# Moving the low halves of the exponentials and of the gated product from GpSimd to VectorE

## The chip, the cores and the metric

The kernel runs on one core of one Trainium2 chip. The time is the device time of one execution in microseconds (us); lower is better. Beside it the profile gives the span, from the first to the last instruction of the program. In the views, PE is TensorE's matmuls, PEld its weight loads, DVE is VectorE, ACT is ScalarE, POOL is GpSimd and SP is SyncE, from whose queue most transfers are issued. L561 is line 561 of the kernel.

## The reference

Three layers follow each other. All inputs and outputs are float32.

```
def phi(x):                                   # x: q or k, 8 batches, 8 heads, 576 rows, 64 wide
    proj = einsum('bhsd,df->bhsf', x, w_phi)  # 128 features
    proj = proj - max(abs(proj), axis=-1)
    return concatenate([exp(proj), exp(-proj)])
q_p, k_p = phi(q), phi(k)
kv, z = einsum('bhsf,bhsd->bhfd', k_p, v), sum(k_p, axis=2)
attn = einsum('bhsf,bhfd->bhsd', q_p, kv) / (einsum('bhsf,bhf->bhs', q_p, z)[..., None] + 1e-6)

x = attn as (4608 tokens, 512)
x = ((x @ w1) * (x @ w2)) @ w3 @ w_out        # d_ff = 1024

e = argmax(x @ w_gate)                        # one of 8 experts for each token
out = softmax(x @ w_gate)[e] * (relu(x @ e_w1[e]) @ e_w2[e])
```

## The kernel before

Every matmul operand is kept as two float16 halves. The high half is the rounded value and the low half is what rounding left, so that three float16 matmuls (high by high, high by low, low by high) stand for one precise product.

**Stages.** Up to about 1225 us the kernel does attention, the gated layer and the preparation of all weights side by side; after that come the experts, where PE has nearly all the work. In the first part four units (pairs of batches) are taken in turn. For each unit there are four calls of `group` (two heads each, attention) and, behind them in due time and beside the next unit's attention, three of `x_prep` and `moe1` (the gated layer, 384 tokens each). The integer arithmetic that turns the raw 64-bit weights into float32 (`conv64`, L214 to L218) runs up to about 190 us.

**The order.** Each step is filed with a due time from the table `O` (`k_lo=0.75`, `q_lo=8.3`, `g_lo=1.2` and so on) and the steps are issued in that order. A scheduler under the kernel then arranges the queue of each engine, by its own estimate of how long each instruction takes and of when its operands are ready. Each engine works through its own queue strictly in order, and semaphores hold an instruction until its operands are there.

**The steps that matter here.** `exp16` (L554, L556) writes an exponential twice on ACT: as float16 into `hl[:, 0]` (tiles `k1`, `q1`, `q2`) and as float32 into `e1`, of which there are three buffers. `exp_lo` (L561) subtracts the one from the other and writes the low half `hl[:, 1]`. It is called 18 times in a group, 6 for the keys and 12 for the queries. In `moe1`, `g_mul` (L817, DVE) multiplies the two projections into `gf`, `g_hi` (L821, ACT) rounds it into `gt`, and `g_lo` (L824) writes the low half; there are 8 of each in a call of `moe1`.

Around them on DVE stand `k_max` (L566), `k_sub` (L572) and `q_max` (L644), which read matmul results from PSUM; `split` (L491, L493), which makes the halves of the queries and keys; `k_c2` (L609), `v_lo` (L540), and the low half of the experts' weights (L325). In `q_add`, L711 and L712 take the numerators `nm` out of PSUM into `nx`; in `q_x`, L719, L720, L721 and L723 divide by the denominators. The PSUM tiles `nm`, `pv` (L521), `pk`, `pq`, `pe` and others share one buffer (tag `ts`, one slot), so that PE can begin on the next only when DVE has read the one before.

```
V.tensor_tensor(nx[:, h], nm[:, :, 0, :], w[:, h].unsqueeze(2).to_broadcast([P, 3, D + 1]), op=ALU.mult)
V.tensor_tensor(nx[:, h], nx[:, h], nm[:, :, 1, :], op=ALU.add)
V.tensor_tensor(rec, nx[:, :, :, D:D + 1], st["ep"][:, :, 3 * c:3 * c + 3].unsqueeze(3), op=ALU.add)
```

Of the kernel before, what the change touches and what calls it, by code (L numbers as in the profile page):

```python
# [14 lines left out]
ALU = mybir.AluOpType  # L15
# [49 lines left out]
def kernel(  # L65
# [16 lines left out]
    V, A, G, T = nc.vector, nc.scalar, nc.gpsimd, nc.tensor  # L82
# [386 lines left out]
    def group(ui, g, T0):  # L469
# [4 lines left out]
        st = {}  # L474
# [83 lines left out]

        def exp_lo(key):
            hl, e1 = st[key]  # L560
            G.tensor_tensor(hl[:, 1], e1, hl[:, 0], op=ALU.subtract)  # L561

        def k_max(h, c):
            if c == 0:
# [162 lines left out]
        for h in range(2):  # L727
            tv = T0 + 3 * h
            for fn in (v_load, v_norm, v_sum, v_scale, v_hi, v_lo, k_s1, k_s2, k_s3, kv_hi, kv_lo):
                at(tv + O[fn.__name__], fn, h)  # L730
            for c in range(3):
                tk = T0 + 3 * h + c
                at(tk + O["k_proj"], proj, "kf", h, c)
                for fn in (k_max, k_sub, k_exp, k_c1, k_c2, k_b):
                    at(tk + O[fn.__name__], fn, h, c)
                at(tk + O["k_lo"], exp_lo, ("k1", h, c))
        for c in range(3):
            tq = T0 + c
            at(tq + O["k_split"], split, "kf", c)
            at(tq + O["k_trans"], trans, "kf", c)  # L740
            at(T0 + O["q_sc"] * c + O["q_split"], split, "qf", c)
            at(T0 + O["q_sc"] * c + O["q_trans"], trans, "qf", c)
            for h in range(2):
                at(T0 + O["q_proj"] + O["q_pc"] * c + O["q_proj_h"] * h, proj, "qf", h, c)
                at(T0 + O["q_max"] + O["q_pc"] * c + O["q_proj_h"] * h, q_max, c, h)
                th = tq + O["q_h"] * h
                for z in range(2):
                    at(th + O["q_lo"] + O["q_lo_z"] * z, exp_lo, ("q", c, h, z))
                for fn in (q_pj, q_exp, q_nm, q_add):
                    at(th + O[fn.__name__], fn, c, h)  # L750
            at(tq + O["q_x"], q_x, c)
# [41 lines left out]
    def moe1(p, c, tk, s):  # L793
# [3 lines left out]
        st = {}  # L797
        gT = []
# [22 lines left out]
            A.copy(gT[m][:, 0, :], st["gf", m])  # L821

        def g_lo(m):
            G.tensor_tensor(gT[m][:, 1, :], st["gf", m], gT[m][:, 0, :], op=ALU.subtract)  # L824

        cw = 256 if last else 260

# [118 lines left out]
        for m in range(8):  # L946
            t = tk + m * s
            at(t, ab, m, 0)
            at(t + 0.5 * s, ab, m, 1)
            for fn in (a_out, g_mul, g_hi, g_lo):  # L950
                at(t + O[fn.__name__], fn, m)
# [278 lines left out]
```

## Time and profile before

| | before |
|---|---|
| median of 3 runs | 1670.81 us (1669.16 to 1676.45) |
| the profiled execution | 1671.89 us |
| its span | 1670.1 us |
| mean granted TensorE clock | 0.943 of full speed |
| PE busy | 1429.4 us, 86% of the span |
| DVE busy | 971.0 us, 58% |
| ACT busy | 885.9 us, 53% |
| POOL busy | 587.5 us, 35% |

The shares are means over two unlike parts. Before 1225 us DVE and PE are both busy for most of the time and POOL for some 40%; behind it only PE is.

### The profile page before, as it was taken

How to read it: one execution, taken by the hardware profiler on the slowest of the kernel's cores; microseconds unless marked ns; L12 is line 12 of the kernel's file. 1: busy time of each engine (PE TensorE's matmuls, PEld its weight loads, DVE VectorE, ACT ScalarE, POOL GpSimd, SP SyncE). 2: the span in 40 equal slices, each digit the busy share in tenths (PEclk: the TensorE clock that was granted, in tenths of full speed). 3: DMA queues.
4: the chain of work that ended last, by engine and by line, in shares of the span. 5: the costliest groups of instructions: out<-in, count | busy, mean ns of one | idle time of the engine just before them, and what ended most of it. 6: DMA issues, size and time to landing. Idle time of an engine off the chain costs nothing. (4 is left out here: it accounts for less than half of the span.)

```text
span 1670.1 us, 38442 instructions
## 1 busy us (share of the span) xinstructions
PE 1429.4 (86%) x14854; PEld 1029.5 (62%) x14854; DVE 971.0 (58%) x2647; ACT 885.9 (53%) x1979; POOL 587.5 (35%) x875
## 2 busy tenths in 40 slices
PE   5888868889897688977787989978949999999998
PEld 4655545656565465756465757646647777777776
DVE  6999989968878687777786886532421111111111
ACT  4787798766776567767576777433311111111111
POOL 3546553444543425434344354211312111121110
PEclk9998978989999799989988999979979999999999
DMA  6756255554257653493955464974347345646361
GB/s 198 217 143 170 64 142 124 144 150 146 71 152 124 127 157 92 119 157 89 161 157 89 139 121 112 140 248 102 70 145 188 83 77 174 221 130 173 76 172 31
DMA packets 273044, 225.17 MB, mean 135 GB/s; under 512 B 187221, under 2 KB 244825, under 8 KB 271706
## 3 DMA queue, kind: packets, MB, share of 16 engines
q1 hardware_dynamic: 265306, 202.71, 50.8%
q0 software_dynamic: 7552, 19.97, 4.1%
q8 instruction: 118, 1.93, 0.5%
q14 instruction: 68, 0.56, 0.1%
HBM read 261.22 MB, written 53.67 MB: 189 GB/s over the span
## 5 line engine op out<-in xcount | busy, mean ns | idle before, releaser
L806 PE MATMUL pab<-xT,w 128*128 128x384 f16 x768 | 263.5, 343 | 8.7 <-DVE gf L817 5.6
L1132 DVE SCALAR_TENSOR_TENSOR hT<-ph,hT 128x512 f16<-128x512 f32 x80 | 55.3, 691 | 362.0 <-ACT hT L1131 362.0
L807 PE MATMUL pab<-xT,w 128*128 128x384 f16 x768 | 262.8, 342 | 0.0
L808 PE MATMUL pab<-xT,w 128*128 128x384 f16 x768 | 262.6, 342 | 0.0
L1127 PE MATMUL ph<-xTb,wb 128*128 128x128 f16 x1280 | 218.1, 220 | 22.5 <-DMA xTb<-rw 22.5
L1128 PE MATMUL ph<-xTb,wb 128*128 128x128 f16 x1280 | 218.1, 220 | 0.0
L1129 PE MATMUL ph<-xTb,wb 128*128 128x128 f16 x1280 | 218.1, 220 | 0.0
L843 PE MATMUL py<-w,gt 128*128 128x260 f16 (+1 forms) x1728 | 205.5, 275 | 12.4 <-ACT yb L850 9.2
L561 POOL TENSOR_TENSOR q<-e,q 128x384 f16<-128x384 f32 x192 | 188.7, 992 | 65.1 <-ACT e L556 60.8
L843 PEld LDWEIGHTS <-gt 128*128 128x128 f16 x1728 | 166.3, 99 | 36.4 <-issue 9.3
L824 POOL TENSOR_TENSOR gt<-gf,gt 128x384 f16<-128x384 f32 x96 | 96.2, 1003 | 182.0 <-ACT gt L821 176.6
L561 POOL TENSOR_TENSOR k<-e,k 128x384 f16<-128x384 f32 x96 | 96.4, 1004 | 159.3 <-ACT k L554 89.3
L702 PE MATMUL nm<-kvs,q 128*128 128x65 f16 (+1 forms) x1920 | 90.1, 204 | 70.2 <-DVE nx L712 35.9
L1131 ACT ACTIVATE hT<-ph 128x512 f16<-128x512 f32 x80 | 47.8, 597 | 187.1 <-PE ph L1129 187.1
L1127 PEld LDWEIGHTS <-wb 128*128 128x128 f16 x1280 | 125.8, 98 | 27.7 <-DMA xTb<-rw 21.2
L702 PEld LDWEIGHTS <-q 128*128 128x128 f16 (+1 forms) x1920 | 79.0, 107 | 100.1 <-issue 47.3
L325 DVE SCALAR_TENSOR_TENSOR pc<-wf,ess,pc 128x512 f16<-128x512 f32 x128 | 104.6, 834 | 47.2 <-ACT pc L321 47.0
L1128 PEld LDWEIGHTS <-wb 128*128 128x128 f16 x1280 | 125.8, 98 | 4.5
L554 ACT ACTIVATE q<-pjT,nM 128x384 f16<-128x384 f32 x192 | 114.4, 596 | 26.0 <-PE nm L702 19.6
L1129 PEld LDWEIGHTS <-wb 128*128 128x128 f16 x1280 | 125.8, 98 | 0.0
L1150 ACT ACTIVATE ob<-pob,scb 128x512 f32<-128x512 f32 x40 | 27.5, 688 | 183.4 <-PE pob L1148 183.4
L626 PE MATMUL kv<-vs,k 128*128 128x65 f16 x1920 | 90.6, 198 | 37.5 <-ACT k L604 23.3
(255 smaller groups left out, 3483.6 us busy)
## 6 DMA issues: line engine op xcount, KB each, us to landing
wb<-wscr SPq DMA_DIRECT2D x40, 4096.0 KB
wf<-in_moe_w_dram SPq DMA_DIRECT2D x16, 2048.0 KB
wscr<-pc SPq DMA_DIRECT2D x128, 256.0 KB
raw<-in_moe_w_dram SPq DMA_DIRECT2D x32, 512.0 KB
rows_d<-row SPq DMA_DIRECT2D x32, 256.5 KB
kf<-in_k_dram SPq DMA_DIRECT2D x64, 128.0 KB
vf<-in_v_dram SPq DMA_DIRECT2D x64, 128.0 KB
qf<-in_q_dram SPq DMA_DIRECT2D x64, 128.0 KB
```

The source lines that it names most:

```text
L325: V.scalar_tensor_tensor(pc[:, 1, :], st["wf"][:, j * 512:(j + 1) * 512], st["s"][:, 0:1], pc[:, 0, :], op0=ALU.mult, op1=ALU.subtract)
L554: A.activation(hl[:, 0], src, AF.Exp, scale=sgn * ES, bias=bias)
L561: G.tensor_tensor(hl[:, 1], e1, hl[:, 0], op=ALU.subtract)
L702: T.matmul(nm[p0:p1, t, z, :], lhsT=hl[:, a, t, p0:p1], rhs=st["kvs"][:, b, h, z, bb, :], start=(a == b), stop=bool(a), skip_group_check=True)
L806: T.matmul(ps, lhsT=wh, rhs=xT[:, 0, kk], start=(kk == 0), stop=False)
L807: T.matmul(ps, lhsT=wh, rhs=xT[:, 1, kk], start=False, stop=False)
L808: T.matmul(ps, lhsT=wl, rhs=xT[:, 0, kk], start=False, stop=(kk == 3))
L824: G.tensor_tensor(gT[m][:, 1, :], st["gf", m], gT[m][:, 0, :], op=ALU.subtract)
L843: T.matmul(py, lhsT=gT[i][:, a, t * P:(t + 1) * P], rhs=w34[:, i, b, hf, 0:cw], start=(i == 0 and a == b), stop=bool(i == 7 and a))
L1127: T.matmul(ph[:, mm, :], lhsT=wh, rhs=xT[:, 0, kk, :], start=(kk == 0), stop=False)
L1128: T.matmul(ph[:, mm, :], lhsT=wh, rhs=xT[:, 1, kk, :], start=False, stop=False)
L1129: T.matmul(ph[:, mm, :], lhsT=wl, rhs=xT[:, 0, kk, :], start=False, stop=(kk == 3))
```

## The change

The two subtractions are issued by VectorE and no longer by GpSimd. Operands, shapes, due times and buffers stay as they are.

```
         def exp_lo(key):
             hl, e1 = st[key]
-            G.tensor_tensor(hl[:, 1], e1, hl[:, 0], op=ALU.subtract)
+            V.tensor_tensor(hl[:, 1], e1, hl[:, 0], op=ALU.subtract)
...
         def g_lo(m):
-            G.tensor_tensor(gT[m][:, 1, :], st["gf", m], gT[m][:, 0, :], op=ALU.subtract)
+            V.tensor_tensor(gT[m][:, 1, :], st["gf", m], gT[m][:, 0, :], op=ALU.subtract)
```

The scheduler arranges the queues of all engines anew. DVE's queue in the first group, where the first numerators `nm_984` and `nm_1041` are taken out of PSUM (the number behind a name is that of the tile, the same in both programs). Before:

```order
L711 TENSOR_TENSOR nx_1018<-nm_984,wq_880 128x195
L638 SCALAR_TENSOR_TENSOR kvs_672<-kv_759,kvs_672 128x130 x2
L712 TENSOR_TENSOR nx_1018<-nx_1018,nm_984 128x195
L566 TENSOR_REDUCE mk_1025<-pj_1003 128x3
L572 TENSOR_TENSOR pm_1036<-pj_1003,mk_1025 128x384
L711 TENSOR_TENSOR nx_1018<-nm_1041,wq_880 128x195
L712 TENSOR_TENSOR nx_1018<-nx_1018,nm_1041 128x195
```

The same place in the changed kernel:

```order
L711 TENSOR_TENSOR nx_1018<-nm_984,wq_880 128x195
L561 TENSOR_TENSOR q1_1010<-e1_1012,q1_1010 128x384
L712 TENSOR_TENSOR nx_1018<-nx_1018,nm_984 128x195
L566 TENSOR_REDUCE mk_1025<-pj_1003 128x3
L217 SCALAR_TENSOR_TENSOR cx_1027<-w12_91,cx_1027 128x512
L572 TENSOR_TENSOR pm_1036<-pj_1003,mk_1025 128x384
L218 SCALAR_TENSOR_TENSOR w12_91<-w12_91,cx_1027 128x512
L561 TENSOR_TENSOR q2_1014<-e1_1016,q2_1014 128x384
L711 TENSOR_TENSOR nx_1018<-nm_1041,wq_880 128x195
L566 TENSOR_REDUCE mk_1025<-pj_1125 128x3
L712 TENSOR_TENSOR nx_1018<-nx_1018,nm_1041 128x195
```

Two of the moved instructions now stand among the six that empty the two `nm` tiles, one of them inside the pair L711 and L712.

POOL's queue at the same exponentials, before:

```order
L561 TENSOR_TENSOR q2_961<-e1_963,q2_961 128x384
L214 TENSOR_SCALAR cx_1180<-raw_909 128x512
L561 TENSOR_TENSOR q1_1010<-e1_1012,q1_1010 128x384
L533 MEMSET vs_1389 128x10
L534 MEMSET vs_1389 128x10
L561 TENSOR_TENSOR q2_1014<-e1_1016,q2_1014 128x384
```

In the changed kernel POOL goes from the conversions straight to the fills of `vs_1389`:

```order
L214 TENSOR_SCALAR cx_1027<-raw_831 128x512
L533 MEMSET vs_1389 128x10
L534 MEMSET vs_1389 128x10
```

DVE's queue in the third unit, where attention and the gated layer run side by side (`gf_10749` is a gated product, `gt_10773` its halves, `pc` are the experts' weights). Before:

```order
L817 TENSOR_TENSOR gf_10749<-pab_10684,asb_10644 128x384
L711 TENSOR_TENSOR nx_10697<-nm_10723,wq_10250 128x195
L325 SCALAR_TENSOR_TENSOR pc_10714<-wf_10071,ess_10650,pc_10714 128x512
L712 TENSOR_TENSOR nx_10697<-nx_10697,nm_10723 128x195
L325 SCALAR_TENSOR_TENSOR pc_10775<-wf_10071,ess_10650,pc_10775 128x512
L719 TENSOR_TENSOR rec_10753<-nx_10697,epq_10251 128x6
```

The same place in the changed kernel:

```order
L817 TENSOR_TENSOR gf_10749<-pab_10684,asb_10644 128x384
L325 SCALAR_TENSOR_TENSOR pc_10714<-wf_10071,ess_10650,pc_10714 128x512
L711 TENSOR_TENSOR nx_10697<-nm_10723,wq_10250 128x195
L561 TENSOR_TENSOR k1_10744<-e1_10746,k1_10744 128x384
L712 TENSOR_TENSOR nx_10697<-nx_10697,nm_10723 128x195
L824 TENSOR_TENSOR gt_10773<-gf_10749,gt_10773 128x384
L719 TENSOR_TENSOR rec_10753<-nx_10697,epq_10251 128x6
```

The low half of the product stands five rows behind the product itself, and a key's low half stands between L711 and L712.

## Rows read from the trace of the kernel before

**Rows 1.** The page's busy time, share of the span, and instructions.

```profile
PE 1429.4 (86%) x14854; PEld 1029.5 (62%) x14854; DVE 971.0 (58%) x2647; ACT 885.9 (53%) x1979; POOL 587.5 (35%) x875
```

**Rows 2.** Busy time of each engine by stretches of the span (columns named).

```profile
core 0: us, PE busy (x) PEld busy (x) DVE busy (x) ACT busy (x) POOL busy (x), PEclk, DMA share, GB/s
50.00:350.00 300.00, 247.77 (x2482) 168.94 (x2483) 275.11 (x699) 235.97 (x544) 144.92 (x224) 0.90 0.56 147
350.00:1050.00 700.00, 578.48 (x6304) 421.37 (x6302) 534.81 (x1517) 484.96 (x1127) 305.18 (x468) 0.94 0.57 124
```

**Rows 3.** Groups of POOL's instructions: count, busy us, mean ns, idle before.

```profile
L561 POOL TENSOR_TENSOR q<-e,q 128x384 f16<-128x384 f32 x192 | 188.7, 992 | 65.1 <-ACT e L556 60.8 <-issue 1.8
L561 POOL TENSOR_TENSOR k<-e,k 128x384 f16<-128x384 f32 x96 | 96.4, 1004 | 159.3 <-ACT k L554 89.3 <-ACT e L556 69.3
L824 POOL TENSOR_TENSOR gt<-gf,gt 128x384 f16<-128x384 f32 x96 | 96.2, 1003 | 182.0 <-ACT gt L821 176.6 <-issue 5.1
```

**Rows 4.** POOL's busy time (and count) by stretches: twice line 561, then line 824.

```profile
50.00:350.00 300.00, 95.19 (x92) 0.90 0.56 147
350.00:1050.00 700.00, 185.19 (x192) 0.94 0.57 124
350.00:1050.00 700.00, 64.12 (x64) 0.94 0.57 124
```

**Rows 5.** Who waited for whom: us in total, times, longest.

```profile
PE nm L702 <- DVE nx L712: 35.9, 14, 7.5
PE pv L521 <- DVE nx L712: 22.3, 12, 4.1
PE nm L702 <- POOL q L561: 7.0, 12, 1.2
```

**Rows 6.** One tile's instructions: duration ns minimum, median, maximum.

```profile
L572 DVE TENSOR_TENSOR pm<-pj,mk x96: 508/546/558, 27.5 to 1004.4; 128x384 f32<-128x384 f32 x96
L712 DVE TENSOR_TENSOR nx<-nx,nm x96: 339/347/359, 82.0 to 1047.5; 128x195 f32<-128x195 f32 x96
L719 DVE TENSOR_TENSOR rec<-nx,epq x48: 148/167/4601, 86.0 to 1048.2; 128x6 f32<-128x6 f32 x48
L540 DVE SCALAR_TENSOR_TENSOR vs<-vf,vss,vs x32: 870/880/3096, 36.8 to 1003.6; 128x640 f16<-128x640 f32 x32
```

**Rows 7.** Groups of DVE's instructions: count, busy us, mean ns, idle before.

```profile
L719 DVE TENSOR_TENSOR rec<-nx,epq 128x6 f32<-128x6 f32 x48 | 28.9, 601 | 0.8
L540 DVE SCALAR_TENSOR_TENSOR vs<-vf,vss,vs 128x640 f16<-128x640 f32 x32 | 32.8, 1024 | 1.5 <-ACT vs L532 1.4 <-DMA vf<-in_v_dram 0.2
```

**Rows 8.** Timeline at 438 us, DVE and POOL: start, us, instruction.

```profile
438.80 4.60 DVE L719 TENSOR_TENSOR rec<-nx,epq 128x6 f32<-128x6 f32 x1
438.98 1.79 POOL L561 TENSOR_TENSOR q<-e,q 128x384 f16<-128x384 f32 x2
...
441.59 1.78 POOL L561 TENSOR_TENSOR q<-e,q 128x384 f16<-128x384 f32 x2
```

**Rows 9.** Timeline from 575 to 582 us, DVE, POOL and PE.

```profile
575.12 1.34 DVE L493 SCALAR_TENSOR_TENSOR sp<-qf,sp 128x192 f16<-128x192 f32 x2
575.18 2.05 POOL L561 TENSOR_TENSOR q<-e,q 128x384 f16<-128x384 f32 x2 [0.31 <-ACT e L556]
576.66 0.54 DVE L566 TENSOR_REDUCE mk<-pj 128x3 f32<-128x384 f32 x1
577.12 0.34 DVE L712 TENSOR_TENSOR nx<-nx,nm 128x195 f32<-128x195 f32 x1
577.61 0.46 PE L521 MATMUL pv<-ssv,ones 128*128 128x1 f32 x2 [4.12 <-DVE nx L712]
579.16 0.53 PE L808 MATMUL pab<-xT,w 128*128 128x384 f16 x1
580.68 0.62 DVE L493 SCALAR_TENSOR_TENSOR sp<-kf,sp 128x192 f16<-128x192 f32 x2
581.72 0.33 PE L808 MATMUL pab<-xT,w 128*128 128x384 f16 x1
```

## The prediction

> **What bounds the kernel now.** I read the totals first. PE is busy for 86% of the span, DVE for 58%, POOL for 35% [rows 1]; over the whole span no engine but PE seems short of time. The table by stretches corrects that [rows 2]. Between 50 and 350 us DVE is busy for 275.1 of 300 us (92%) and PE for 247.8 (83%), at a granted clock of 0.90. Between 350 and 1050 us DVE is busy for 534.8 of 700 us (76%) and PE for 578.5 (83%) at 0.94. So while attention runs DVE is the fullest engine first and the second fullest later, and the moved work lands on it.
>
> Then I read whom PE waits for. The two longest waits that concern this change are for L712, the instruction that empties the shared PSUM slot: 35.9 us in 14 waits before `nm` and 22.3 us in 12 before `pv`, together 58.2 us [rows 5]. For the instructions to be moved PE waits little: 7.0 us in 12 waits for L561 [rows 5]. GpSimd's own lateness is therefore not what holds the kernel. What it does to DVE may be.
>
> That shows in the durations. L719 handles 6 numbers in a row of a tile; its shortest takes 148 ns, its median 167, its longest 4601 [rows 6]. At the longest, DVE starts L719 at 438.80 us, GpSimd runs five L561 from 438.98 to 443.37, and L719 ends at 443.40 [rows 8]: it stood until the last of them was done. L712 and L572, which take one operand from PSUM, never take more than 359 and 558 ns [rows 6]. So an instruction of DVE with its operands in SBUF can be held by GpSimd, one that reads PSUM is not. The Trainium skill (SBUF — State Buffer, "Who interferes with whom") says that a VectorE instruction with two SBUF inputs and a GpSimd instruction that reads SBUF exclude each other; this trace agrees, with 4601 against 167 ns.
>
> **What the change does, part by part.** *Removed from GpSimd*: 192 + 96 + 96 = 384 instructions, 188.7 + 96.4 + 96.2 = 381.3 us [rows 3]. GpSimd is no bound, so that by itself is worth only part of the 7.0 us above.
>
> *Added to DVE*: the same 384. The trace has no such instruction on DVE. The nearest is L572, also a subtraction of two operands over 128x384: 546 ns from start to end, 508 at least [rows 6]. When something is ready behind an instruction of this length the next starts sooner: L566 (as long) starts at 576.66 and L712 at 577.12, 0.46 us later, though L566 lasts 0.54 [rows 9]. Bounds: 384 x 0.46 = 177 us and 384 x 0.55 = 211 us. DVE mostly has work queued, so I take 0.48 us, which is 184 us. The Trainium skill (VectorE: DVE Perf Modes, "The DRAIN you can't avoid") has the next instruction wait until the pipeline is empty; by that the upper bound would be the price, 211 us, against my 184. The two rows above, which overlap by 0.08 us, speak for the lower.
>
> *Given back to DVE*: the holding ends. I take for each group the mean less the median, times the count. L719: (601 - 167) x 48 = 20.8 us; L540, the smallest of ten groups that I counted: (1024 - 880) x 32 = 4.6 us [rows 6, 7]. The eight between (L493 for queries and for keys, L325, L721, L723, L609, L491 twice) come by the same working to 79 us, together 104 us, or 0.27 us for each instruction moved. The bounds are 0 (if what stays on GpSimd, such as the conversions and the indirect transfers, did the holding) and some 130 us (with the small groups). I take 104, since in the two stretches of timeline that I show it is L561 that holds.
>
> *Sum for DVE*: 184 - 104 = +80 us of work, between 177 - 130 = +47 and +211. It falls mostly into two stretches. From 50 to 350 us stand 92 L561 and some 8 L824, from 350 to 1050 us 192 and 64 [rows 4]. At +0.21 us each (0.48 - 0.27) that is +21 us on 275.1, which makes 296 of 300, and +54 us on 534.8, which makes 589 of 700.
>
> *What of it reaches the end.* Before 350 us DVE would have nearly no gap left. If its gaps could close, nothing would be lost; if its share stayed at 92% (275.1 of 300), the stretch would take 296 / 0.917 = 323 us, 23 longer. I take about half, +10 us. Behind 350 us DVE has gaps, and the question is what happens where PE waits. The timeline at 575 to 582 us shows such a place [rows 9]. Two L493 take 1.34 us at 575.12 while GpSimd runs two L561; L712, which nothing holds, comes late behind them, and PE stands for 4.12 us. At 580.68 two L493 take 0.62 us, so GpSimd costs DVE 0.7 us here; on DVE the two subtractions cost 2 x 0.48 = 1.0 us. Nothing is won. At 438 us five of them hold DVE for 4.4 us and would cost 2.4 [rows 8]; there something is won. Where GpSimd's instructions meet PSUM readers, 0.48 us is simply added. Of PE's 58.2 us of waits for L712 [rows 5] I let a tenth go, -6 us, and of its 7.0 us for L561 one half, since the subtraction takes 0.55 us in place of 0.99: -4 us.
>
> A long stand costs PE more than itself. After the 4.12 us the same matmul takes 0.53 us at 579.16 and 0.33 at 581.72 [rows 9]: PE ran at its lower level (1.2 of 2.4 GHz) in between. I count nothing for it, since nearly as many long stands should stay.
>
> The in-order queue is the last part. GpSimd could wait for ACT without harm; 60.8, 89.3 + 69.3 and 176.6 us of its idle time end with ACT [rows 3]. The same wait on DVE holds what stands behind: in the changed queue L712 stands behind a subtraction that needs ACT, and PE waits for L712. I cost it at nothing, because ACT's exponential is filed well ahead and DVE runs late rather than early; if that cover is gone each wait is paid in full by PE's next use of the PSUM slot.
>
> Sum: +10 - 6 - 4 = 0. The profiled execution took 1671.9 us, 1.1 above the median of the runs (1670.8). I predict **1672 us**.
>
> **The rivals.** *Forecast: it cancels*, 1660 to 1684 us, chance 0.40. For it: the sum above, and the place at 575 us.
>
> *Rival 1, slower: DVE becomes the bound.* Place: 50 to 350 us, and every `nm` behind it. Price: +23 us in the first stretch when DVE's share stays at 92%; behind it, if a quarter of the +54 us lengthens the waits for L712, +13 us, less 10 us won: 1672 + 26 = about 1698; with the lower end of the added work (+47 in place of +80) about 1687. I put it at 1692. It decides as soon as DVE cannot close its gaps between 50 and 350 us. For it: 92% is much, and the price 0.55 would add 27 us. Against it: a held DVE is late by microseconds at a time, a busy one by half of one. Chance 0.33. The skill's drain rule is a case of this rival (DVE's work grows by 107 in place of 80 us; the first stretch by 7 more, some 1679), within its chance and, by the overlapping rows, not likelier than 0.05.
>
> *Rival 2, faster: the long holdings were the cause.* If half of the 58.2 us goes (29 us) and the half-speed stretches behind them shrink (a 4 us stand is followed by some 3.4 us at half speed, 1.7 us lost; ten fewer, 17 us, of which I take a third), with 4 us from L561 and +10 us lost early: 1672 - 29 - 6 + 6 = about 1645. For it: one L719 of 4.60 us. Against it: the place at 575 us. Chance 0.27.
>
> That the change does not do what it says is no rival: the queues show the subtractions on DVE and gone from GpSimd.
>
> **How the numbers follow.** A measurement of this kernel can tell about 0.5%, 8 us: below 1662 faster, above 1679 slower. The forecast's 0.40 I split 0.10 below, 0.22 within, 0.08 above. Faster 0.27 + 0.10 = 0.37; same 0.22; slower 0.33 + 0.08 = 0.41. The range reaches into both rivals until 2 in 10 are left out: 1642 to 1702. The ends of the unknown costs lie outside it (+211 us if nothing is given back, all of it at the end: 1883), because PE, not DVE, is the fuller engine behind 350 us.
>
> **What would show it.** Right: 384 subtractions on DVE at 0.5 to 0.56 us; L719's mean near its median; DVE about 80 us busier in all; PE's waits for L712 between 45 and 65 us. Rival 1: DVE above 96% between 50 and 350 us, ACT waiting for L561 to free `e1` buffers, longer waits for L712. Rival 2: waits for L712 below 35 us and a clock above 0.95 in both stretches. Wrong altogether: if the newly arranged queues of PE or SP, which I did not cost, move a step of the gated layer or a transfer by more than all this.

## The result and the profile after

The change made the kernel faster: 1648.6 us (median of 4 runs, 1648.2 to 1653.9) against 1673.6 us for the kernel before on the same chip (4 runs, 1669.2 to 1677.6). The ratio is 0.9862, 95% interval 0.9843 to 0.9882. I had forecast 1672 us, no change to speak of.

The later runs were on chips on which the kernel before takes 1651 to 1654 us, so each run there is compared by its ratio to the kernel before on the same chip, and traces only with traces of equal footing.

The page of the changed kernel, busy time, share of the span and instructions:

```profile
PE 1428.4 (86%) x14850; PEld 1032.2 (62%) x14854; DVE 1001.4 (61%) x3031; ACT 881.7 (53%) x1979; POOL 226.9 (14%) x491
```

Beside [rows 1], POOL lost 360.6 us and DVE gained only 30.4, where I had summed +80. PE's busy time is the same; the profiled execution (1653.9 us, span 1652.2) is shorter because PE idles less.

The stretches (columns as in [rows 2]):

```profile
50.00:350.00 300.00, 253.65 (x2494) 176.65 (x2496) 275.30 (x786) 235.34 (x543) 45.26 (x121) 0.86 0.51 134
350.00:1050.00 700.00, 593.54 (x6424) 429.19 (x6422) 573.88 (x1852) 496.67 (x1161) 74.78 (x220) 0.94 0.66 132
```

Between 50 and 350 us DVE's share stayed where it was, 275.3 of 300 us; between 350 and 1050 us it rose from 534.8 to 573.9. PE's clock did not rise: 0.86 and 0.94, after 0.90 and 0.94.

The moved instructions, and L719 and L723 that stand beside them (groups of DVE's instructions, then one tile's durations in ns):

```profile
L561 DVE TENSOR_TENSOR q<-e,q 128x384 f16<-128x384 f32 x192 | 106.1, 556 | 18.4 <-ACT e L556 17.9
L561 DVE TENSOR_TENSOR k<-e,k 128x384 f16<-128x384 f32 x96 | 54.0, 562 | 22.9 <-ACT e L556 20.6 <-ACT k L554 2.0
L824 DVE TENSOR_TENSOR gt<-gf,gt 128x384 f16<-128x384 f32 x96 | 52.9, 551 | 20.8 <-ACT gt L821 19.9 <-issue 0.6
```

```profile
L719 DVE TENSOR_TENSOR rec<-nx,epq x48: 152/159/166, 87.5 to 1023.9; 128x6 f32<-128x6 f32 x48
L723 DVE TENSOR_TENSOR xn<-nx,rec x48: 544/552/1012, 89.2 to 1025.8; 128x384 f32<-128x384 f32 x48
```

A subtraction takes 551 to 562 ns on DVE, as the 546 ns of L572 had suggested. L719 never takes more than 166 ns now; before it took up to 4601 [rows 6]. The new waits for ACT that I had costed at nothing are there (17.9 + 20.6 + 19.9 us of DVE's idle time), and they did not decide. PE's waits for L712 (us in total, times, longest):

```profile
PE nm L702 <- DVE nx L712: 37.4, 18, 15.8
PE pv L521 <- DVE nx L712: 2.0, 2, 1.8
```

Together 39.4 us, after 58.2 [rows 5]: nearly all of the waits before `pv` went. PE's waits for the moved instructions on POOL, 7.0 us for L561 [rows 5], are gone.

Other waits moved as well, and by as much. Before, PE waited at `kv`, the product of keys and values, for the halves of the keys' second exponential (L604 on ACT, L609 on DVE):

```profile
PE kv L626 <- ACT k L604: 23.3, 7, 14.4
PE kv L626 <- DVE k L609: 9.4, 10, 1.7
```

In the changed kernel these fell from 32.7 to 6.1 us, and three waits that were nearly absent before came up:

```profile
PE kv L626 <- DVE k L609: 3.2, 6, 1.2
PE kv L626 <- ACT k L604: 2.9, 5, 1.6
PE pab L806 <- ACT asb L813: 16.1, 5, 7.1
PE pj L547 <- DMA Tkf<-sp: 10.9, 2, 6.2
PE pj L547 <- ACT e L556: 9.9, 4, 5.4
```

### The profile page after: what moved, and what is told of

It reads as the page before. It is cut to its first block, busy times and chain, and to the rows that moved or that the text cites. A ratio compares the mean times of both kernels' runs of the same rounds, so it can differ in the third digit from the quotient of the medians.

```text
span 1652.2 us, 38216 instructions
## 1 busy us (share of the span) xinstructions
PE 1428.4 (86%) x14850; PEld 1032.2 (62%) x14854; DVE 1001.4 (61%) x3031; ACT 881.7 (53%) x1979; POOL 226.9 (14%) x491
## 5 line engine op out<-in xcount | busy, mean ns | idle before, releaser
L806 PE MATMUL pab<-xT,w 128*128 128x384 f16 x768 | 258.8, 337 | 26.1 <-ACT asb L813 16.1
L807 PE MATMUL pab<-xT,w 128*128 128x384 f16 x768 | 258.8, 337 | 0.0
L808 PE MATMUL pab<-xT,w 128*128 128x384 f16 x768 | 258.3, 336 | 0.0
L843 PE MATMUL py<-w,gt 128*128 128x260 f16 (+1 forms) x1728 | 213.6, 278 | 16.5 <-ACT yb L850 12.1
L843 PEld LDWEIGHTS <-gt 128*128 128x128 f16 x1728 | 166.6, 100 | 43.3 <-issue 13.3
L702 PE MATMUL nm<-kvs,q 128*128 128x65 f16 (+1 forms) x1920 | 86.7, 201 | 41.3 <-DVE nx L712 37.4
L1146 PE MATMUL pob<-wb,hT 128*128 128x512 f16 x320 | 121.3, 379 | 0.0
L1147 PE MATMUL pob<-wb,hT 128*128 128x512 f16 x320 | 121.3, 379 | 0.0
L1148 PE MATMUL pob<-wb,hT 128*128 128x512 f16 x320 | 121.3, 379 | 0.0
L321 ACT ACTIVATE pc<-wf,ess 128x512 f16<-128x512 f32 x128 | 88.8, 726 | 57.2 <-DMA wscr<-pc 50.1
L556 ACT ACTIVATE e<-pjT,nM 128x384 f32<-128x384 f32 x192 | 116.0, 604 | 5.8 <-DVE q L561 5.8
L702 PEld LDWEIGHTS <-q 128*128 128x128 f16 (+1 forms) x1920 | 76.9, 104 | 66.1 <-issue 38.0
```

The lines of the kernel that those rows point to most:

```text
L556: A.activation(e1, src, AF.Exp, scale=sgn * ES, bias=bias)
L702: T.matmul(nm[p0:p1, t, z, :], lhsT=hl[:, a, t, p0:p1], rhs=st["kvs"][:, b, h, z, bb, :], start=(a == b), stop=bool(a), skip_group_check=True)
L806: T.matmul(ps, lhsT=wh, rhs=xT[:, 0, kk], start=(kk == 0), stop=False)
L807: T.matmul(ps, lhsT=wh, rhs=xT[:, 1, kk], start=False, stop=False)
L808: T.matmul(ps, lhsT=wl, rhs=xT[:, 0, kk], start=False, stop=(kk == 3))
L843: T.matmul(py, lhsT=gT[i][:, a, t * P:(t + 1) * P], rhs=w34[:, i, b, hf, 0:cw], start=(i == 0 and a == b), stop=bool(i == 7 and a))
```

## Experiments

Three theories were tried. *Holding*: GpSimd's subtractions held DVE's SBUF instructions, and the release of these is the gain. *Order*: the queues were arranged anew, and the gain is an accident of that. *Latency*: PE gets the low halves themselves sooner. All ratios are to the kernel before on the same chip, with the 95% interval.

**Does arrangement alone move the time?** The kernel before with one due time moved:

```
-    k_lo=0.75
+    k_lo=0.85
```

> The kernel before with one due time moved (k_lo from 0.75 to 0.85), engines as they were: the queues are arranged anew and nothing else. Holding theory: within 0.5% of before. Order theory: arrangement alone moves the time by as much as the change did, 1% or more in either direction.

Measured: 1652.3 us, ratio 1.000 (0.9975 to 1.0024). This run does not try the order theory, because nothing was rearranged. Read from the two traces in order of start, TensorE's 14,854 matmuls and weight loads, DVE's 2647 instructions and those of ACT and POOL stand in the same order as in the kernel before, by operation, tile and shape. What the run gives is a second trace of the kernel before, on the chip of the next three runs. The order theory is tried by the runs below, in which the order was kept and the time moved.

**The release by itself.** The kernel before, with GpSimd writing in place of subtracting:

```
-            G.tensor_tensor(hl[:, 1], e1, hl[:, 0], op=ALU.subtract)
+            G.memset(e1, 0.0); G.memset(hl[:, 1], 0.0)
...
-            G.tensor_tensor(gT[m][:, 1, :], st["gf", m], gT[m][:, 0, :], op=ALU.subtract)
+            G.memset(st["gf", m], 0.0); G.memset(gT[m][:, 1, :], 0.0)
```

> The kernel before, with each of the 384 subtractions on GpSimd replaced by two fills on GpSimd (of e1 or gf, and of the low half): the low halves are zeros, a part of the computation that is left out. GpSimd is about as busy, waits for the same things and VectorE gets no new work, but GpSimd no longer reads SBUF. Holding theory: this is the gain of the release alone, at least that of the change: ratio to before 0.97 to 0.985, L719's mean below 200 ns. Order theory: the queues of the other engines stay nearly those of before, so the ratio is within 0.5% of 1.

Measured: 1587.1 us, ratio 0.9615 (0.9593 to 0.9637), 66 us below before and more than I had expected. (The profiled execution took 1577.0 us, 10 less than the median.) GpSimd is still busy for 512 us. Its page, and L719:

```profile
PE 1406.0 (89%) x14854; PEld 1022.8 (65%) x14854; DVE 857.3 (54%) x2647; ACT 881.3 (56%) x1979; POOL 511.9 (32%) x1259
```

```profile
L719 DVE TENSOR_TENSOR rec<-nx,epq x48: 146/159/252, 82.7 to 961.7; 128x6 f32<-128x6 f32 x48
```

DVE executes the same 2647 instructions as before. To compare on one footing I take the run with the shifted due time, which is the kernel before on this chip:

```profile
PE 1425.7 (86%) x14854; PEld 1027.7 (62%) x14854; DVE 965.4 (58%) x2647; ACT 886.1 (54%) x1979; POOL 587.3 (36%) x875
```

DVE's busy time falls from 965.4 to 857.3 us: 108.1 us were holding. PE's waits for L712 fall from 53.2 us (28.5 and 24.7) to 28.8:

```profile
PE nm L702 <- DVE nx L712: 19.4, 13, 5.4
PE pv L521 <- DVE nx L712: 9.4, 8, 1.9
```

The order of the matmuls is nearly that of the kernel before: 52 of 14,854 stand elsewhere, by tile and shape. The order theory expected a ratio within 0.5% of 1 here, so it is refuted as the account of the release. The zeros don't shorten the matmuls: one of L702 takes 190 ns at least and 194 in the median, with them and without. A fill is not free of holding, though. L491, which reads a single tile in SBUF, still takes up to 1430 ns in this run:

```profile
L491 DVE TENSOR_SCALAR sp<-kf x48: 346/360/1430, 11.5 to 859.2; 128x384 f16<-128x384 f32 x48
```

**The change on the same chip.**

> The changed kernel on the chip of this call, for its ratio beside the others and its trace: 0.984 to 0.988 by the first measurement. The two halves of the change alone came to 0.9888 and 0.9885 on another chip; if that holds here, the halves do not add up.

Measured: 1630.8 us, ratio 0.9886 (0.9857 to 0.9915). Its page:

```profile
PE 1431.5 (88%) x14854; PEld 1033.1 (63%) x14854; DVE 1001.1 (61%) x3031; ACT 882.7 (54%) x1979; POOL 228.4 (14%) x491
```

From the fills (857.3) to the change (1001.1) DVE gained 143.8 us for 384 subtractions, 0.37 us each, and the time rose by 1630.8 - 1587.1 = 44 us. So the change is two large terms: -66 us of release and +44 us of added work. (The low halves' arithmetic is absent in the first, so this split is that of two programs, not of one execution. The +44 also holds what the new order does: about 1,500 of the 14,854 matmuls stand elsewhere, and no run parts the two.)

**More work on DVE.** Each subtraction made twice:

```
             V.tensor_tensor(hl[:, 1], e1, hl[:, 0], op=ALU.subtract)
+            V.tensor_tensor(e1, e1, hl[:, 0], op=ALU.subtract)
...
             V.tensor_tensor(gT[m][:, 1, :], st["gf", m], gT[m][:, 0, :], op=ALU.subtract)
+            V.tensor_tensor(st["gf", m], st["gf", m], gT[m][:, 0, :], op=ALU.subtract)
```

> The changed kernel with each moved subtraction made twice on VectorE (the second into e1 or gf, no longer needed): 384 more instructions on VectorE and nothing on GpSimd. My sum counted 0.48 us for each (184 us) and let +10 us reach the end. If added work on VectorE is cheap, as the holding theory now needs: ratio to before 0.985 to 1.0. If VectorE is the bound once it is this full: 1.02 to 1.06. Order theory: no forecast.

Measured: 1767.4 us, ratio 1.0716 (1.0672 to 1.076). This is above the upper of my two brackets. DVE's busy time:

```profile
PE 1481.3 (84%) x14854; PEld 1054.7 (60%) x14854; DVE 1175.4 (67%) x3415; ACT 889.7 (50%) x1979; POOL 227.5 (13%) x491
```

The second 384 cost 174.3 us of DVE and 137 us of the time, three times what the first 384 cost. Added work was cheap for the first 384 and dear for the next; rival 1 was real, one step further on. That it was cheap because DVE had gaps is my reading. The matmuls' order moved here too, in about 1,500 places against the change.

**Holding put back.** The changed kernel, with GpSimd making each subtraction once more, and the same with two fills in its place:

```
             V.tensor_tensor(hl[:, 1], e1, hl[:, 0], op=ALU.subtract)
+            G.tensor_tensor(e1, e1, hl[:, 0], op=ALU.subtract)       # reading
...
             V.tensor_tensor(hl[:, 1], e1, hl[:, 0], op=ALU.subtract)
+            for _ in range(2):
+                G.memset(e1, 0.0)                                     # writing
```

(`gf` in the same way.)

> The changed kernel, and behind each moved subtraction GpSimd makes the same subtraction once more, into the float32 tile that is no longer needed (e1 or gf): GpSimd's 384 reading instructions are back, VectorE keeps its own. Holding theory: VectorE is held again by some 100 us in all, L719's mean is above 400 ns, and the time goes up by 20 to 45 us, to 1670 to 1695 us. Order theory: VectorE's and TensorE's own instructions are those of the changed kernel, so about 1649 us, within 8. Latency theory: 1649 us.

> The same as the run with GpSimd's repeated subtractions, but GpSimd only writes: two fills of the same float32 tile, together about as long as one subtraction, behind the same waits. Holding theory: instructions that only write do not hold VectorE's two-operand ones, L719's mean stays below 250 ns, 1645 to 1660 us. If it is the mere presence of work on GpSimd (or the later release of e1 and gf) that costs, it comes out like the reading run. Order theory: 1649 us, within 8.

Measured: reading 1741.7 us, ratio 1.0532 (1.0497 to 1.0568); writing 1632.8 us, ratio 0.9867 (0.9818 to 0.9915). The reading run costs far more than the 20 to 45 us that I expected, some 110 us above the writing one, and the writing one costs nothing. GpSimd's main groups in the two (the inserted lines shift the numbers by one and two):

```profile
L562 POOL TENSOR_TENSOR e<-e,q 128x384 f32<-128x384 f32 x192 | 203.0, 1065 | 112.1 <-DVE q L561 86.9 <-DVE rec L722 5.9 <-DVE rec L720 5.7
```

```profile
L563 POOL MEMSET e<- 128x384 f32 x576 | 241.1, 427 | 300.7 <-DVE k L561 132.6 <-DVE q L561 91.1 <-DVE vss L194 12.8
```

Two fills are about as long as a subtraction (2 x 0.43 against 1.07 us). The pages, reading and then writing:

```profile
PE 1463.5 (84%) x14854; PEld 1044.0 (60%) x14854; DVE 1154.9 (66%) x3031; ACT 892.7 (51%) x1979; POOL 636.4 (37%) x875
```

```profile
PE 1425.5 (88%) x14854; PEld 1029.9 (63%) x14854; DVE 1007.3 (62%) x3031; ACT 883.6 (54%) x1979; POOL 538.1 (33%) x1259
```

DVE has the same 3031 instructions in both and is busy for 147.6 us more when GpSimd reads. My sign for it, a mean of L719 above 400 ns, did not come: that mean is 170 ns. It was the new subtractions on DVE that were held, with a mean of 754 ns in place of 556:

```profile
L561 DVE TENSOR_TENSOR q<-e,q 128x384 f16<-128x384 f32 x192 | 143.9, 754 | 9.3 <-ACT e L556 8.6 <-issue 0.4
```

What held DVE is GpSimd reading SBUF, not GpSimd working. The later release of `e1` and `gf` is in both runs; it explains no busy time of DVE, and ACT waits for GpSimd to release `e1` for 23.7 us in the reading run and 13.3 us in the writing one. The matmuls stand in the order of the changed kernel in the reading run and within 7 places of it in the writing one. So the order theory, which expected 1649 us (0.986) of the reading run, is refuted as the cause of the gain, and so is the latency theory.

**Parts of the change.** Exponentials alone, the product alone, and two splits (`key[0]` tells keys from queries):

```
+            V.tensor_tensor(hl[:, 1], e1, hl[:, 0], op=ALU.subtract)       # exponentials alone: g_lo stays on G
...
+            V.tensor_tensor(gT[m][:, 1, :], st["gf", m], gT[m][:, 0, :], op=ALU.subtract)   # product alone: exp_lo stays on G
...
+            (V if key[0] == "k1" else G).tensor_tensor(hl[:, 1], e1, hl[:, 0], op=ALU.subtract)   # keys and product
...
+            (G if key[0] == "k1" else V).tensor_tensor(hl[:, 1], e1, hl[:, 0], op=ALU.subtract)   # queries and product
```

> Only the exponentials' low halves (288 instructions) go to VectorE; the product's (96) stay on GpSimd. Holding theory (the gain is that GpSimd's subtractions no longer hold VectorE's SBUF instructions): the 25 us are shared out roughly by instructions, so about -19 us, some 1655 us, and the mean of L719 falls most of the way from 601 ns to 160 ns. Order theory (the gain is an accident of how the queues were arranged anew): no such sharing; anything between 1640 and 1680 us. Latency theory (the gain is that PE gets the low halves sooner): PE's 7 us of waits for L561 go, 1665 us.

> Only the product's low halves (96 instructions) go to VectorE. Holding theory: about -6 us, some 1667 us, and L719's mean stays above 450 ns. Order theory: anything between 1640 and 1680 us. Latency theory: the short tail behind the last attention group gains 1 to 3 us, 1671 us.

> Keys' and product's low halves (192) on VectorE, the queries' (192) on GpSimd. The product's 96 alone gave 0.9885 and all 384 gave 0.9862 and 0.9886. If release is won first and the price of added work grows with VectorE's load: 0.98 to 0.987, better than either. If the halves simply share one gain: 0.988, the same.

> Queries' and product's low halves (288) on VectorE, the keys' (96) on GpSimd: 0.98 to 0.988, between the run with keys and product and the whole change, if it goes by the number of instructions moved. The queries' stand right at q_add and q_x, where L719 was held for up to 4.6 us; if it is the place that counts, this one is the best of the three.

| on VectorE | instructions moved | ratio to before | interval |
|---|---|---|---|
| exponentials | 288 | 0.9888 | 0.9849 to 0.9927 |
| product | 96 | 0.9885 | 0.9847 to 0.9923 |
| keys and product | 192 | 0.9887 | 0.9852 to 0.9921 |
| queries and product | 288 | 0.9820 | 0.9790 to 0.9849 |
| all (the change) | 384 | 0.9886 and 0.9862 | 0.9857 to 0.9915 and 0.9843 to 0.9882 |

The parts do not add up. The 96 of the product gain 19 us, where a share by count gives 6; keys and product came to 0.9887, where a price that grows with DVE's load had let me expect 0.98 to 0.987. With the product alone L719 is still held for up to 3167 ns:

```profile
L719 DVE TENSOR_TENSOR rec<-nx,epq x48: 148/167/3167, 86.5 to 1014.7; 128x6 f32<-128x6 f32 x48
```

Among the splits the queries with the product do best, as the place beside `q_add` and `q_x` suggested; that the place is the reason is not shown. A price of added work that grows with DVE's load would explain that the whole gains no more than a part; the runs don't show it for each part. Each split also orders the matmuls anew (232 to 1,149 places against before), so how the parts share the gain may hang on order too.

**The first unit left on GpSimd.**

```
+            (G if ui == 0 else V).tensor_tensor(hl[:, 1], e1, hl[:, 0], op=ALU.subtract)
```

> The changed kernel, but the first unit's 72 exponentials' low halves stay on GpSimd (before some 260 us, where VectorE is fullest). In the traces of one chip the first unit's last output stands at 255.5 us with GpSimd and at 265.1 us with the change, which is 9.6 us lost there and more won later. Holding theory with a price that depends on how full VectorE is: the 9.6 us come back and the rest stays, ratio to before 0.980 to 0.984. If the change's gain later hangs on its early part, or on the arrangement as a whole: 0.986 to 1.0.

Measured: 1615.6 us, ratio 0.9782 (0.9766 to 0.9799), the fastest version with all of the work in it, faster than either kernel: about 15 us below the change by the ratios. The start of the last L723 of the first unit, in the run that stands for before, in the change, in the fills and in this version:

```profile
254.94 0.55 DVE L723 TENSOR_TENSOR xn<-nx,rec 128x384 f32<-128x384 f32 x1
```

```profile
264.52 0.55 DVE L723 TENSOR_TENSOR xn<-nx,rec 128x384 f32<-128x384 f32 x1
```

```profile
238.93 0.55 DVE L723 TENSOR_TENSOR xn<-nx,rec 128x384 f32<-128x384 f32 x1
```

```profile
256.62 0.55 DVE L723 TENSOR_TENSOR xn<-nx,rec 128x384 f32<-128x384 f32 x1
```

The change loses 9.6 us in the first unit, and this version gets 7.9 of them back. The end of the last unit's attention, in the run that stands for before, in the change, in the fills and in this version:

```profile
1037.99 0.55 DVE L723 TENSOR_TENSOR xn<-nx,rec 128x384 f32<-128x384 f32 x1
```

```profile
1008.24 0.55 DVE L723 TENSOR_TENSOR xn<-nx,rec 128x384 f32<-128x384 f32 x1
```

```profile
964.48 0.55 DVE L723 TENSOR_TENSOR xn<-nx,rec 128x384 f32<-128x384 f32 x1
```

```profile
996.54 0.55 DVE L723 TENSOR_TENSOR xn<-nx,rec 128x384 f32<-128x384 f32 x1
```

From the first unit's end to the last's: before 783.1 us, the change 743.7 (39.3 less), the fills 725.6 (57.5 less), this version 739.9. So about half of what it wins over the change comes in the first unit and the rest behind it; why the rest comes was not tried.

**Both splits together.**

```
+            (G if ui == 0 or key[0] == "k1" else V).tensor_tensor(hl[:, 1], e1, hl[:, 0], op=ALU.subtract)
```

> Both of the better splits together: the queries' and the product's low halves on VectorE, but not before the first unit's attention is over; the keys' stay on GpSimd throughout. If the two savings are independent (0.9782 for leaving the first unit on GpSimd, and 0.982 against 0.9886 for leaving the keys), 0.972 to 0.976. If both save the same VectorE time, 0.978, no better than the better one. If the keys' instructions on GpSimd hold VectorE beside the gated layer, 0.98 or worse.

Measured: 1620.1 us, ratio 0.9814 (0.9787 to 0.9841). The two savings do not add. The ratio falls under the last of the three forecasts, but that the keys' instructions hold DVE beside the gated layer was not tried by itself.

## Why the prediction was wrong

**What held.** That DVE is held by GpSimd, and only in instructions that take their operands from SBUF: shown, by the reading and writing runs. The size of the holding: 104 us summed, 108.1 measured. The sign of the early stretch: +10 us summed, and the first unit ends 9.6 us later on one chip and 4.9 in the first pair of traces (259.7 and 264.6 us), with DVE's share hardly changed. The sum meant 50 to 350 us, though, and there the loss does not last: at the end of the second unit (510.3 us before, 505.0 after, on the one chip) the change already leads. That GpSimd's own lateness and DVE's new waits for ACT would not decide: so it was.

**What was mis-sized in the sum for DVE.** The price of an added subtraction: 0.48 us summed, 0.37 us of busy time measured between the fills and the change (0.45 for the second 384). DVE's net came to +36 us there (965.4 to 1001.1) and +30 in the first pair of traces, below my lower bound of +47. A likely reason is that an added instruction also fills the pause between two that depend on each other; I had priced it between two that don't. One place shows it. Before, L723 started 0.20 us behind L721, whose result it needs:

```profile
443.66 0.17 DVE L721 TENSOR_TENSOR rec<-rec,svi 128x6 f32<-128x6 f32 x1
443.86 0.56 DVE L723 TENSOR_TENSOR xn<-nx,rec 128x384 f32<-128x384 f32 x1
```

In the change a subtraction stands between such a pair and lengthens it to 0.55 us, by 0.35:

```profile
263.97 0.16 DVE L721 TENSOR_TENSOR rec<-rec,svi 128x6 f32<-128x6 f32 x1
264.05 0.55 DVE L561 TENSOR_TENSOR k<-e,k 128x384 f16<-128x384 f32 x1
264.52 0.55 DVE L723 TENSOR_TENSOR xn<-nx,rec 128x384 f32<-128x384 f32 x1
```

How many of the 384 stand so was not counted; what the fills still held of L491 lowers the 0.37 too.

**The step that failed.** "Of PE's 58.2 us of waits for L712 [rows 5] I let a tenth go, -6 us". It rested on the place at 575 us, which I called "Nothing is won", and on taking two microseconds of DVE, one held and one worked, to be worth the same at the end. Both were wrong. At that place I counted 0.7 us of holding, of the two L493. The instructions ahead of them were held too:

```profile
572.85 0.66 DVE L721 TENSOR_TENSOR rec<-rec,svi 128x6 f32<-128x6 f32 x1
573.85 1.02 POOL L824 TENSOR_TENSOR gt<-gf,gt 128x384 f16<-128x384 f32 x1 [0.36 <-ACT gt L821]
574.02 1.07 DVE L491 TENSOR_SCALAR sp<-qf 128x384 f16<-128x384 f32 x1
```

L721 takes 166 ns in the median and L491 360, so some 1.9 us were held between L721 and L712. In the fills DVE runs the same instructions there in the same order, and PE's stand of 4.12 us (4.07 in the run that stands for before) is 0.94:

```profile
529.36 0.35 PE L521 MATMUL pv<-ssv,ones 128*128 128x1 f32 x2 [0.94 <-DVE nx L712]
```

In all, the waits for L712 fell by 18.8 us in the first pair of traces, and on the other chip from 53.2 us to 28.8 by the release alone and to 29.9 (27.8 + 2.1) by the change, not to some 48; the rows of the change there are:

```profile
PE nm L702 <- DVE nx L712: 27.8, 16, 8.6
PE pv L521 <- DVE nx L712: 2.1, 2, 1.8
```

The release returned 108 us of DVE and 66 us of the time, 0.61 each; the first 384 subtractions took 144 us of DVE and 44 us of the time, 0.30 each. (By the profiled executions, 1655.7, 1577.0 and 1630.4 us, it is 0.73 and 0.37.) Behind the first unit the change won 39.3 us, where most of my -6 and -4 belong. Why a held microsecond costs twice a worked one is not settled. What the traces offer: a hold lasts until GpSimd has finished a row of instructions and can stand right ahead of what PE waits for, while the scheduler places an added subtraction where its own estimate finds DVE free. That it knows of no hold is my guess.

**A term that the sum left out.** PE's waits at `kv` were 32.7 us before, nearly as large as those before `nm`, and the prediction has no word on them. They fell by 26.6 us, and new waits for ACT and a transfer took that back and more (16.1 + 10.9 + 9.9 us). By the release alone they fell only from 32.9 to 23.0 us, so most of their fall comes with the added work or the new order; which of the two is open.

**The rivals.** Rival 2 was right in its sign and in its cause, with 1645 us (its terms add up to 1643; 1648.6 measured), but not in its account. The clock did not rise in the change (0.943 before, 0.936 after), so the third of 17 us that I gave to it was not there; in the fills it did, to 0.957 after 0.946. The waits for L712 fell by a third in the first pair of traces and by 44% on the other chip, where rival 2 had half. Rival 1's mechanism is real in the first unit and takes over with the next 384 instructions.

## What to carry to other kernels

Where GpSimd and VectorE work side by side, read the maximum beside the median of a small VectorE instruction: 4601 against 167 ns is time that the busy share counts as work. Price held time apart from work: here a held microsecond cost twice as much at the end as a worked one. Try it by letting GpSimd only write, and make sure that the queues keep their order while you do. Then move the GpSimd instructions that read SBUF off it where VectorE still has gaps, and leave them where it has none: the best version here left only the first unit's 72 exponentials on GpSimd.

## What the runs showed of the hardware

A VectorE instruction that is held need not be let in between two of GpSimd's: L719 stood for five subtractions in a row, 4.60 us [rows 8]. GpSimd's fills, 128x384 float32 in 427 ns, did not hold L719, which has two operands in SBUF, for long (at most 252 ns when fills stood in place of the subtractions), but L491, with one, took up to 1430. 384 GpSimd instructions that read cost VectorE 147.6 us of busy time beside 768 that only write.
